# Tile-local attention into a routed mixture of experts: the order of TensorE's work in an attention turn, the way k is read, and the first loads

## The chip, the cores and the metric

One core of a Trainium2 chip runs the whole program. The metric is the device time of one execution in microseconds (us); lower is better. The core has five engines that run their own instruction streams and wait for each other by semaphores: TensorE (PE in the profile, with its weight loads as PEld), VectorE (DVE), ScalarE (ACT), GpSimd (POOL) and SyncE (SP), which here only issues transfers. Sixteen DMA engines carry the transfers.

## The reference

```
# q, k, v: (8, 8, 576, 64); chunks of 64 tokens attend within themselves
scores = matmul(q_c, k_c.T) / sqrt(64)
attn   = exp(scores - max(scores));  attn /= sum(attn) + 1e-9
x      = matmul(attn, v_c)                 -> 4608 tokens x 512
noisy  = x @ w_gate + log1p(exp(x @ w_noise)) * noise
top2   = the two largest of 8 experts per token, softmax over the two
out   += top2_w[k] * (relu(x @ w1[e]) @ w2[e])   for both experts e
```

All tensors are fp32.

## The kernel before, in words

The 4608 tokens are 36 tiles of 128 tokens. A tile is two chunks of 64 tokens for each of 8 heads, and heads go in pairs (hp, 0 to 3). The program has two stages that overlap a little.

**Attention stage.** The function `attend(it)` is one *turn*; turns 0 to 35 each start one tile, and turns 36 to 40 finish the pipeline. A turn is software-pipelined over several tiles. In the program's order it issues on TensorE: `pv(it-2)` (the product of the transposed probabilities with v, L427), `p_trans(it-1)` (four 128x128 transposes of the probabilities, L417), `scores(it+1)` (q times k, L400), `x_trans(it-3)` (four transposes of the finished rows of x, L443). Every fourth turn adds `gate_mm` (L455) and, a turn later, `gate_sum` (L468); the routing of the previous group of tiles adds a few small products (L523, L525) in a step called "pe". The products `scores` and `pv` give 64 rows of the result at a time, so two of them stand side by side in the array (the profile writes 128*64); transposes and `gate_sum` use the full array (128*128), `gate_mm` four columns of 32 (128*32). An fp32 product is two instructions in the trace, a transpose one: x16 for `scores` and `pv`, x4 for the transposes.

VectorE does for each turn the maximum (L405) and the subtraction (L410) for tile it, the three steps of the normalization of tile it-2 (L432, L435, L438), and up to six steps of routing. ScalarE copies the transposed probabilities out of PSUM (L419, inside `p_trans`), does the exponential (L413), copies the transposed x (L449), and the copies and functions of gate and routing. GpSimd scatters finished rows to their experts' slots by indirect DMA (L590); each of the at most two scatters of a turn is held back by a one-element copy (L588) from the maximum or from the reciprocal of that turn. In even turns from 12 to 26 it also splits weights (L125).

PSUM bank use: scores alternate between banks 0 and 1, the transposed probabilities have bank 2, `pv` banks 3 and 4, the transposed x bank 5. So `pv` of the next tile needs the normalization of the last one done, and `scores` of a tile needs the subtraction of the tile two before.

The inputs come in pairs of tiles: `load_qk(j)` and `load_v(j)` fill rings of three buffers (KB, VB, QB). KB holds k in two halves by parity of the head, with zeros in the other rows, so one product does a pair of heads. `scores` reads it as `p k h`: for each key position first the one head, then the other, from two places of the buffer. The scores so stand in PSUM in the order (group, key, head), and VectorE reads them through the view `by_head`. KB and VB are cleared once at the start (L358), before the first loads; the constants are made ahead of that. All loads are issued by SP, in the program's order.

**Expert stage.** From turn 36 on, TensorE runs the blocks of the experts (L267), three tiles of tokens at a time, each product in three parts for precision. Blocks 0 and 1 of expert 0 are gathered early, when the scatters of groups 3 and 6 have landed (`gather`, on SP); the remaining attention and routing turns are woven into block 0 by hooks.

Of the kernel before, what the change touches and what calls it, by code (L numbers as in the profile page):

```python
# [8 lines left out]
FT = mybir.dt.float32  # L9
# [10 lines left out]
P = 128  # L20
# [29 lines left out]
def kernel(ctx, tc, qT, kT, vh, wgn, noise, w1, w2, out, caps=CAPS):  # L50
# [4 lines left out]

    slots = dram.tile([LROWS * NE, ROW], FT, name="slots")
    by_slot = slots.rearrange("(r e) c -> r e c", e=NE)


    jp = consts.tile([P, P], FT, name="jp")  # L60
    nc.gpsimd.iota(jp, pattern=[[1, P]], base=0, channel_multiplier=-1, allow_small_or_imprecise_dtypes=True)
    ident = consts.tile([P, P], FT, name="ident")
    nc.vector.tensor_scalar(ident, jp, 0.0, None, op0=OP.is_equal)
    before = consts.tile([P, P], BF, name="before")
    nc.vector.tensor_scalar(before, jp, 0.0, None, op0=OP.is_gt)
    ones = consts.tile([P, P], BF, name="ones")
    nc.vector.memset(ones, 1.0)
    spacer = consts.tile([1, 1], FT, name="spacer")
    e_row = consts.tile([P, NE], FT, name="e_row")
    nc.gpsimd.iota(e_row, pattern=[[1, NE]], base=0, channel_multiplier=0, allow_small_or_imprecise_dtypes=True)  # L70
    col = consts.tile([P, 1], FT, name="col")
    nc.gpsimd.iota(col, pattern=[[0, 1]], base=0, channel_multiplier=1, allow_small_or_imprecise_dtypes=True)
    slot8 = consts.tile([P, NLIST], FT, name="slot8")
    nc.gpsimd.iota(slot8, pattern=[[NE * P, NLIST]], base=NE - 1, channel_multiplier=NE, allow_small_or_imprecise_dtypes=True)
    tok = consts.tile([P, NT], FT, name="tok")
    nc.gpsimd.iota(tok, pattern=[[P, NT]], base=P, channel_multiplier=1, allow_small_or_imprecise_dtypes=True)

    lii = consts.tile([P, 2, NT], I32, name="lii")
    order = consts.tile([1, NE], I32, name="order")
    cape = consts.tile([P, NE], FT, name="cape")  # L80
    caprow = consts.tile([P, NE], FT, name="caprow")
    top = consts.tile([P, NE], FT, name="top")
    place_e = consts.tile([P, NE], FT, name="place_e")
    for c in sorted(set(caps[1:])):
        n = caps.index(c, 1)
        nc.vector.memset(caprow[:, n:n + caps[1:].count(c)], float(c))
    nc.vector.memset(caprow[:, 0:1], float(caps[0]))
    sel = consts.tile([P, 16], FT, name="sel")
    nc.vector.tensor_add(sel, ident[:, 0:16], ident[:, 32:48])
    nc.vector.tensor_add(sel, sel, ident[:, 64:80])  # L90
    nc.vector.tensor_add(sel, sel, ident[:, 96:112])
    run8 = consts.tile([P, NE], FT, name="run8")
    nc.vector.tensor_copy(run8, e_row)


    wpool = {1: ctx.enter_context(tc.tile_pool(name="weights1", bufs=1))}
# [256 lines left out]
    VB = [vs.tile([P, 2, 2, 2, 4, 65], FT, name=f"vb{n}") for n in range(RING)]  # L353
    QB = {}
    HALF = (slice(0, 64), slice(64, 128))
    for n in range(RING):
        for t in (KB[n], VB[n]):
            (nc.vector if n == 0 else nc.gpsimd).memset(t, 0.0)  # L358

    def load_qk(j):  # L360
        if j < NT // 2:
# [5 lines left out]
    def load_v(j):  # L367
        if j < NT // 2:
            for h in range(2):
                nc.sync.dma_start(VB[j % RING][h::2, h], vh[HALF[h], 2 * j:2 * j + 2])  # L370

    nc.scalar.preload_act_table_set("natural_log_exp_and_others")
    for j in range(2):
        load_qk(j)
        load_v(j)
    wg = consts.tile([P, ND, 32], FT, name="wg")
    nc.sync.dma_start(wg, wgn)
    nz = consts.tile([P, NT, NE], FT, name="nz")
# [7 lines left out]

    PR, PT, XS, XT, RC = {}, {}, {}, {}, {}
    by_head = lambda a: a.rearrange("p (g k h) -> p g h k", g=4, h=2)
    sco = [by_head(PS[:, b, :]) for b in range(2)]

    def x_at(t):
        u, r = divmod(t, 4)
# [4 lines left out]
    def scores(t):  # L397
        for hp in range(4):
            for q in HALF:
                nc.tensor.matmul(PS[q, t % 2, hp * P:(hp + 1) * P], QB[t // 2][:, t % 2, hp, q],  # L400
                                 KB[t // 2 % RING][:, :, t % 2, hp, q].rearrange("p h k -> p k h"), start=True, stop=True)

    def soft_max(t):
        mx = work.tile([P, 4, 2], FT, name="mx", bufs=2)
# [10 lines left out]
    def p_trans(t):  # L415
        for hp in range(4):
            nc.tensor.transpose(PS[:, 2, hp * P:(hp + 1) * P], PR[t][:, hp * P:(hp + 1) * P], ident)  # L417
        PT[t] = work.tile([P, 4, P], FT, name="pts", bufs=2)
        nc.scalar.activation(PT[t].rearrange("p a b -> p (a b)"), PS[:, 2, :], AF.Copy)  # L419

# [241 lines left out]
    def attend(it):  # L662
        STEPS = 6
        if it % 2:
            load_qk((it - 1) // 2 + 3)
        if it % 2 == 0 and it >= 4:
            load_v((it - 4) // 2 + 3)
        if it in (5, 7):
            for r in range(CLEAN + 64 * (it // 2 - 2), CLEAN + 64 * (it // 2 - 1), 16):
                nc.sync.dma_start(slots[r * NE:(r + 16) * NE, 0:USED], zero)  # L670
        if it == 7:
            nc.sync.dma_start(slots[(CLEAN + P) * NE:NLIST * P * NE, CODE:USED].rearrange("(p r) c -> p r c", p=P),
                              zero[:, 0:3 * (NLIST * P - CLEAN - P) // 16].rearrange("p (r c) -> p r c", c=3))
        if it in (9, 11, 13, 15):
            w_load(0, 1, (it - 9) // 2)
        if it == 32:
            zero_out(8)
        if it in (29, 31, 33, 35):
            w_load(0, 2, (it - 29) // 2)
        next_turn()  # L680
        if it == 0:
            scores(0)
        if 0 <= it - 2 < NT:
            pv(it - 2)
        if 0 <= it - 1 < NT:
            p_trans(it - 1)
        if it + 1 < NT:
            scores(it + 1)
        if 0 <= it - 3 < NT:
            x_trans(it - 3)  # L690
        gated = it - 4 >= 0 and (it - 4) % 4 == 3
        if gated:
            gate_mm((it - 4) // 4)
        step_route("pe")
        if it - 5 >= 0 and (it - 5) % 4 == 3:
            gate_sum((it - 5) // 4)
            if grp_of[it - 5] != grp_of.get(it - 4):
                r = route(grp_of[it - 5])
                routing.append([r, next(r)])
        if it < NT:  # L700
            mx = soft_max(it)
            soft_sub(it, mx)
            scatter(1, mx[0:1, 0, 0:1])
            soft_exp(it)
        if 0 <= it - 3 < NT:
            x_copy(it - 3)
        if gated:
            gate_copy((it - 4) // 4)
        step_route("act")
# [12 lines left out]
        if it in range(12, 28, 2):  # L722
            w_split(0, 1, *wq.pop(0), eng=nc.gpsimd)
# [241 lines left out]
```

## Time and profile before

| | |
|---|---|
| median of 3 runs | 1003.32 us (1001.34 to 1003.67) |
| profiled execution | 995.33 us, its span 993.5 us |
| TensorE busy | 970.2 us (98%) |
| VectorE, ScalarE, GpSimd busy | 463.2, 284.0, 225.6 us |
| mean granted TensorE clock | 0.996 |

Times of instructions come from the one profiled execution and count from the start of its span. A row of a timeline has the start, the time from the first start to the last end of what is merged in it, engine, line, operation, output and inputs, shapes and the count; idle time before it and what ended it stand in brackets. Matmuls overlap in the pipeline, so the step from one row's start to the next row's start says more of the cost than a row's own length.

### The profile page before, as it was taken

How to read it: one execution, taken by the hardware profiler on the slowest of the kernel's cores; microseconds unless marked ns; L12 is line 12 of the kernel's file. 1: busy time of each engine (PE TensorE's matmuls, PEld its weight loads, DVE VectorE, ACT ScalarE, POOL GpSimd, SP SyncE). 2: the span in 40 equal slices, each digit the busy share in tenths (PEclk: the TensorE clock that was granted, in tenths of full speed). 3: DMA queues.
4: the chain of work that ended last, by engine and by line, in shares of the span. 5: the costliest groups of instructions: out<-in, count | busy, mean ns of one | idle time of the engine just before them, and what ended most of it. 6: DMA issues, size and time to landing. Idle time of an engine off the chain costs nothing.

```text
span 993.5 us, 16063 instructions
## 1 busy us (share of the span) xinstructions
PE 970.2 (98%) x5788; PEld 853.4 (86%) x5788; DVE 463.2 (47%) x1042; ACT 284.0 (29%) x595; POOL 225.6 (23%) x320
## 2 busy tenths in 40 slices
PE   5999999999999999999999999999999999999996
PEld 4777778798899888988998899889988998899885
DVE  5778876333535442544344434443344334433311
ACT  2556554112233221312231323132213221322100
POOL 3026666831100111021012101210111111111112
PEclk9999999999999999999999999999999999999999
DMA  7989999959621652276116622572264226402213
GB/s 267 311 272 343 317 375 398 293 159 148 177 39 33 148 136 35 36 143 150 36 24 134 164 45 31 103 182 48 32 151 132 47 32 152 112 13 33 32 22 44
DMA packets 96834, 132.92 MB, mean 134 GB/s; under 512 B 23376, under 2 KB 56528, under 8 KB 96752
## 3 DMA queue, kind: packets, MB, share of 16 engines
q1 hardware_dynamic: 80320, 93.54, 31.9%
q0 software_dynamic: 16432, 38.33, 19.3%
q8 instruction: 46, 0.75, 0.3%
q14 instruction: 36, 0.29, 0.1%
HBM read 81.69 MB, written 50.13 MB: 133 GB/s over the span
## 4 chain that ended last, share of the span: by engine, by line
PE 94%; DMA 1%; DVE 1%; issue 1%; POOL 1%; ACT 0%; SPq 0%; POOLq 0%; ACTq 0%
PE PS L267 79%; PE PS L400 5%; PE PS L427 4%; PE PS L417 2%; PE PS L443 2%; PE PS L312 1%; PE PS L455 1%; PE PS L468 1%; DMA slots<-xs,lii 1%; POOL out L234 0%; PE PS L250 0%; DMA kb<-in_kT 0%; POOL slots L590 0%; DMA xg<-slots 0%; DVE xl L258 0%
## 5 line engine op out<-in xcount | busy, mean ns | idle before, releaser
L234 POOL DMA_INDIRECT out<-o,lid x77 | 119.9, 1557 | 662.0 <-DVE o L297 642.3
L267 PE MATMUL PS<-xh,w1h 128*128 128x384 f32 (+2 forms) x768 | 261.7, 341 | 0.5 <-DVE hl L289 0.3
L267 PE MATMUL PS<-xl,w1h 128*128 128x384 f32 (+2 forms) x768 | 260.4, 339 | 0.2 <-DVE xl L258 0.2
L267 PE MATMUL PS<-xh,w1l 128*128 128x384 f32 (+2 forms) x768 | 260.4, 339 | 0.0
L267 PE MATMUL PS<-w2h,hh 128*128 128x512 f32 x584 | 228.6, 392 | 0.0
L267 PE MATMUL PS<-w2h,hl 128*128 128x512 f32 x584 | 228.5, 391 | 0.0
L267 PE MATMUL PS<-w2l,hh 128*128 128x512 f32 x584 | 228.5, 391 | 0.0
L286 ACT ACTIVATE hh<-PS 128x384 fp32r<-128x384 f32 (+2 forms) x192 | 95.2, 496 | 463.0 <-PE PS L267 462.9
L289 DVE SCALAR_TENSOR_TENSOR hl<-PS,hh 128x384 fp32r<-128x384 f32 (+2 forms) x192 | 108.7, 566 | 178.1 <-ACT hh L286 146.4
L297 DVE TENSOR_SCALAR o<-PS,lwt 128x512 f32<-128x512 f32 x77 | 57.7, 749 | 231.1 <-PE PS L267 223.0
L267 PEld LDWEIGHTS PS<-xh,w1h 128*128 128x128 f32 x768 | 144.2, 188 | 7.4 <-issue 4.6
L267 PEld LDWEIGHTS PS<-xl,w1h 128*128 128x128 f32 x768 | 144.2, 188 | 2.1 <-DVE xl L258 0.5
L267 PEld LDWEIGHTS PS<-xh,w1l 128*128 128x128 f32 x768 | 144.2, 188 | 1.0
L267 PEld LDWEIGHTS PS<-w2h,hl 128*128 128x128 f32 x584 | 109.7, 188 | 23.4
L267 PEld LDWEIGHTS PS<-w2h,hh 128*128 128x128 f32 x584 | 109.7, 188 | 22.5
L267 PEld LDWEIGHTS PS<-w2l,hh 128*128 128x128 f32 x584 | 109.5, 188 | 22.7
L590 POOL DMA_INDIRECT slots<-xs,lii x72 | 71.1, 988 | 17.6 <-issue 16.9
L257 ACT ACTIVATE xh<-y 128x512 fp32r<-128x512 f32 x67 | 41.2, 614 | 92.7 <-DVE y L254 92.7
L258 DVE TENSOR_TENSOR xl<-y,xh 128x512 fp32r<-128x512 f32 x67 | 45.0, 671 | 48.2 <-ACT xh L257 48.2
L400 PE MATMUL PS<-kb,qb 128*64 128x128 f32 x576 | 48.8, 315 | 10.1 <-DMA kb<-in_kT 10.1
L400 PEld LDWEIGHTS PS<-kb,qb 128*64 128x64 f32 x576 | 38.3, 143 | 15.9 <-issue 15.4
L254 DVE STREAM_TRANSPOSE y<-xg 128x512 f32<-128x512 f32 x67 | 45.6, 680 | 0.0
(126 smaller groups left out, 692.6 us busy)
## 6 DMA issues: line engine op xcount, KB each, us to landing
st<-in_w SPq DMA_DIRECT2D x36, 512.0 KB
xg<-slots SPq DMA_DIRECT2D x252, 64.0 KB
st<-in_w SPq DMA_DIRECT2D x112, 128.0 KB
out<-zero SPq DMA_DIRECT2D x37, 256.0 KB
vb<-in_vh SPq DMA_DIRECT2D x36, 260.0 KB
qb<-in_qT SPq DMA_DIRECT2D x36, 256.0 KB
kb<-in_kT SPq DMA_DIRECT2D x36, 256.0 KB
xg<-slots SPq DMA_DIRECT2D x9, 256.0 KB
```

Of the source, the lines that this page charges most:

```text
L234: s = nc.gpsimd.indirect_dma_start(out=out, out_offset=bass.IndirectOffsetOnAxis(ap=rows_of(i, j)[0:r], axis=0), in_=o[0:r], in_offset=Non ...
L254: nc.vector.transpose(y[:, 0:4 * r], x[:, 0:4 * r])
L257: nc.scalar.activation(oh, src, AF.Copy)
L258: nc.vector.tensor_sub(ol, src, oh.bitcast(FT))
L267: nc.tensor.matmul(p, a, b, start=first and n == 0, stop=last and n == 2)
L286: nc.scalar.activation(hh[:, 0:n], p, AF.Relu)
L289: nc.vector.scalar_tensor_tensor(hl[:, 0:n], p, 0.0, hh[:, 0:n].bitcast(FT), op0=OP.max, op1=OP.subtract)
L297: nc.vector.tensor_scalar(o[0:r], p[0:r], w, None, op0=OP.mult)
L400: nc.tensor.matmul(PS[q, t % 2, hp * P:(hp + 1) * P], QB[t // 2][:, t % 2, hp, q], KB[t // 2 % RING][:, :, t % 2, hp, q].rearrange("p h k ...
L417: nc.tensor.transpose(PS[:, 2, hp * P:(hp + 1) * P], PR[t][:, hp * P:(hp + 1) * P], ident)
L427: nc.tensor.matmul(PS[q, 3 + hp // 2, o:o + 130], PT[t][:, hp, q], VB[t // 2 % RING][:, :, t % 2, c, hp, :], start=True, stop=True)
L590: s = nc.gpsimd.indirect_dma_start(out=slots, out_offset=bass.IndirectOffsetOnAxis(ap=lii[:, k, t0 + r:t0 + r + 1], axis=0), in_=XS[(t0 + ...
```

## The change

1. In a turn TensorE now does `scores(it+1)`, `pv(it-2)` and, where due, `gate_mm`; then `p_trans(it-1)` and `x_trans(it-3)`; then `gate_sum` and the "pe" step of routing.
2. ScalarE's copy of the transposed probabilities is a function of its own, `p_copy`, and stands behind the exponential of the turn.
3. `scores` reads k as it lies, 64 keys of one head and then 64 of the other, so the scores stand in PSUM as (group, head, key), and the view `sco` follows; the probabilities are still written as (group, key, head).
4. At the start VectorE clears the first tile's half of KB[0], then the second's, then VB[0]; the first pair's q comes by four half-size loads on SP, its k by four on ScalarE's queue; constants are made after that; GpSimd clears KB[1] first and the rest after its constants.

```diff
-    for n in range(RING):
-        for t in (KB[n], VB[n]):
-            (nc.vector if n == 0 else nc.gpsimd).memset(t, 0.0)
...
+    for a in range(2):
+        nc.vector.memset(KB[0][:, :, a], 0.0)
+    nc.gpsimd.memset(KB[1], 0.0)
+    nc.vector.memset(VB[0], 0.0)
+    QB[0] = loads.tile([P, 2, 4, P], FT, name="qb", bufs=RING)
+    for a in range(2):
+        for h in range(2):
+            nc.sync.dma_start(QB[0][h::2, a], qT[HALF[h], a])
+            nc.scalar.dma_start(KB[0][h::2, h, a], kT[HALF[h], a])
     nc.scalar.preload_act_table_set("natural_log_exp_and_others")
-    for j in range(2):
-        load_qk(j)
-        load_v(j)
+    load_v(0)
...
+    nc.gpsimd.memset(VB[1], 0.0)
+    for t in (KB[2], VB[2]):
+        nc.gpsimd.memset(t, 0.0)
+    load_qk(1)
+    load_v(1)
...
-    sco = [by_head(PS[:, b, :]) for b in range(2)]
+    sco = [PS[:, b, :].rearrange("p (g h k) -> p g h k", g=4, h=2) for b in range(2)]
...
-                                 KB[t // 2 % RING][:, :, t % 2, hp, q].rearrange("p h k -> p k h"), start=True, stop=True)
+                                 KB[t // 2 % RING][:, :, t % 2, hp, q], start=True, stop=True)
...
             nc.tensor.transpose(PS[:, 2, hp * P:(hp + 1) * P], PR[t][:, hp * P:(hp + 1) * P], ident)
+
+    def p_copy(t):
         PT[t] = work.tile([P, 4, P], FT, name="pts", bufs=2)
...
+        if it + 1 < NT:
+            scores(it + 1)
         if 0 <= it - 2 < NT:
             pv(it - 2)
-        if 0 <= it - 1 < NT:
-            p_trans(it - 1)
-        if it + 1 < NT:
-            scores(it + 1)
-        if 0 <= it - 3 < NT:
-            x_trans(it - 3)
         gated = it - 4 >= 0 and (it - 4) % 4 == 3
         if gated:
             gate_mm((it - 4) // 4)
-        step_route("pe")
+        if 0 <= it - 1 < NT:
+            p_trans(it - 1)
+        if 0 <= it - 3 < NT:
+            x_trans(it - 3)
...
+        step_route("pe")
         if it < NT:
             mx = soft_max(it)
             soft_sub(it, mx)
             scatter(1, mx[0:1, 0, 0:1])
             soft_exp(it)
+        if 0 <= it - 1 < NT:
+            p_copy(it - 1)
```

TensorE's order in turns 6 and 7 before: L427 is `pv`, L417 `p_trans`, L400 `scores`, L443 `x_trans`.

```order
L427 MATMUL PS<-vb_146,pts 64x130 x8
L417 MATMUL PS<-ident,pr 128x128 x4
L400 MATMUL PS<-kb_141,qb 64x128 x8
L443 MATMUL PS<-ident,xs 128x128 x4
L427 MATMUL PS<-vb_146,pts 64x130 x8
L417 MATMUL PS<-ident,pr 128x128 x4
L400 MATMUL PS<-kb_142,qb 64x128 x8
L443 MATMUL PS<-ident,xs 128x128 x4
L455 MATMUL PS<-xt,wg 32x512 x4
```

The same turns now, to the first transposes of turn 7: L408 is `scores`, L437 `pv`, L465 `gate_mm`, L425 `p_trans`, L453 `x_trans`.

```order
L408 MATMUL PS<-kb_108,qb 64x128 x8
L437 MATMUL PS<-vb_113,pts 64x130 x8
L425 MATMUL PS<-ident,pr 128x128 x4
L453 MATMUL PS<-ident,xs 128x128 x4
L408 MATMUL PS<-kb_109,qb 64x128 x8
L437 MATMUL PS<-vb_113,pts 64x130 x8
L465 MATMUL PS<-xt,wg 32x512 x4
L425 MATMUL PS<-ident,pr 128x128 x4
```

Before, products of 64 columns and transposes of 128 alternate, four changes in a turn; now the two products stand together and the two transposes, two changes in a turn.

ScalarE in two such turns before, with the copy of the probabilities (L419) ahead of the exponential (L413) and the copy of x (L449):

```order
L419 ACTIVATE pts<-PS 128x512
L413 ACTIVATE pr<-pr 128x512
L449 ACTIVATE xt<-PS 128x4x128
L419 ACTIVATE pts<-PS 128x512
L413 ACTIVATE pr<-pr 128x512
L449 ACTIVATE xt<-PS 128x4x128
```

And now, with the exponential (L421) ahead of the two copies (L429, L459):

```order
L421 ACTIVATE pr<-pr 128x512
L429 ACTIVATE pts<-PS 128x512
L459 ACTIVATE xt<-PS 128x4x128
L421 ACTIVATE pr<-pr 128x512
L429 ACTIVATE pts<-PS 128x512
L459 ACTIVATE xt<-PS 128x4x128
```

The exponential and the copy of the probabilities have changed places.

SP's first loads before, to the second pair of tiles (kb_142):

```order
L364 DMA qb<-in_qT 64x1024
L365 DMA kb_141<-in_kT 64x1024
L364 DMA qb<-in_qT 64x1024
L365 DMA kb_141<-in_kT 64x1024
L370 DMA vb_144<-in_vh 64x1040 x2
L364 DMA qb<-in_qT 64x1024
L365 DMA kb_142<-in_kT 64x1024
L364 DMA qb<-in_qT 64x1024
L365 DMA kb_142<-in_kT 64x1024
```

And now, to the second pair (kb_109); the first pair's k is issued by ScalarE, as its first four instructions:

```order
L340 DMA qb<-in_qT 64x512 x4
L331 DMA vb_111<-in_vh 64x1040 x2
L325 DMA qb<-in_qT 64x1024
L326 DMA kb_109<-in_kT 64x1024
L325 DMA qb<-in_qT 64x1024
L326 DMA kb_109<-in_kT 64x1024
```

The first pair's q stands in four halves at the head of SP's queue, and none of SP's first four loads follows a cleared buffer any more.

## Rows read from the trace of the kernel before

**Rows 1.** The page: busy time by engine, and the chain's shares by line.

```profile
PE 970.2 (98%) x5788; PEld 853.4 (86%) x5788; DVE 463.2 (47%) x1042; ACT 284.0 (29%) x595; POOL 225.6 (23%) x320
...
PE PS L267 79%; PE PS L400 5%; PE PS L427 4%; PE PS L417 2%; PE PS L443 2%; PE PS L312 1%; PE PS L455 1%; PE PS L468 1%; DMA slots<-xs,lii 1%; POOL out L234 0%; PE PS L250 0%; DMA kb<-in_kT 0%; POOL slots L590 0%; DMA xg<-slots 0%; DVE xl L258 0%
```

**Rows 2.** Timeline of PE, turns 6 and 7 (start, length, what).

```profile
32.84 1.30 PE L400 MATMUL PS<-kb,qb 128*64 128x128 f32 x16
34.08 0.66 PE L443 MATMUL PS<-ident,xs 128*128 128x128 f32 x4
34.66 1.11 PE L427 MATMUL PS<-vb,pts 128*64 128x130 f32 x16
35.70 0.66 PE L417 MATMUL PS<-ident,pr 128*128 128x128 f32 x4
36.29 1.31 PE L400 MATMUL PS<-kb,qb 128*64 128x128 f32 x16
```

**Rows 3.** Timeline, PE in turn 35, which has no scores.

```profile
145.60 0.66 PE L417 MATMUL PS<-ident,pr 128*128 128x128 f32 x4
...
146.09 0.60 PE L443 MATMUL PS<-ident,xs 128*128 128x128 f32 x4
...
146.62 1.07 PE L455 MATMUL PS<-xt,wg 128*32 128x512 f32 x8
```

**Rows 4.** Lines L400 and L427, matmuls, 29.2 to 145 us (shortest/median/longest ns).

```profile
L400 PE MATMUL PS<-kb,qb x480: 298/300/348, 29.4 to 143.6; 128*64 128x128 f32 x160
...
L427 PE MATMUL PS<-vb,pts x472: 272/273/326, 31.2 to 145.0; 128*64 128x130 f32 x158
```

**Rows 5.** Groups by line, DVE, 30 to 170 us (busy, mean ns | idle before).

```profile
L438 DVE TENSOR_TENSOR xs<-PS,rc 128x512 f32<-128x512 f32 x33 | 22.8, 692 | 1.8 <-DVE rc L435 0.6 <-DMA slots<-xs,lii 0.2
...
L410 DVE TENSOR_TENSOR pr<-PS,mx 128x512 f32<-128x512 f32 x30 | 20.8, 692 | 1.7
```

**Rows 6.** Windows: length, busy PE, PEld, DVE, ACT, POOL, clock, DMA share, GB/s.

```profile
69.59:85.28 15.69, 15.69 (x185) 12.17 (x189) 13.04 (x49) 9.46 (x21) 11.29 (x17) 1.00 0.97 337
...
116.68:132.38 15.70, 15.70 (x186) 12.19 (x189) 12.75 (x51) 8.43 (x19) 10.83 (x19) 1.00 0.99 343
...
150.00:175.00 25.00, 22.85 (x160) 20.09 (x161) 16.64 (x85) 11.72 (x28) 15.83 (x25) 1.00 1.04 396
```

**Rows 7.** Timeline of POOL: two scatters in a row, and a split.

```profile
78.16 1.00 POOL L590 DMA_INDIRECT slots<-xs,lii  x1 [0.16 <-issue]
79.17 0.18 POOL L588 COPY spacer<-rc 1x1 f32<-1x1 f32 x1
79.50 0.99 POOL L590 DMA_INDIRECT slots<-xs,lii  x1 [0.16 <-issue]
...
83.20 1.28 POOL L125 TENSOR_TENSOR w1l<-st,w1h 128x512 fp32r<-128x512 f32 x1
```

**Rows 8.** Timeline of the start: clearing, loads, first scores.

```profile
0.73 0.58 SPq L364 DMA_DIRECT2D qb<-in_qT  x1
...
2.60 1.76 DVE L358 MEMSET kb<- 128x2048 f32 x1
...
4.75 1.79 DVE L358 MEMSET vb<- 128x2080 f32 x1 [0.38 <-issue]
...
10.07 3.68 PE L400 MATMUL PS<-kb,qb 128*64 128x128 f32 x32 [10.07 <-DMA kb<-in_kT]
...
15.27 1.98 PE L400 MATMUL PS<-kb,qb 128*64 128x128 f32 x16
```

**Rows 9.** The chain that ended last: first load, turn 4, last early scatter and gather.

```profile
5.56 4.38 DMA kb<-in_kT
...
24.39 1.04 PE PS L427 x16
...
181.14 5.37 DMA slots<-xs,lii
...
186.53 2.94 DMA xg<-slots
```

**Rows 10.** Timeline of PE around the gather of block 1.

```profile
189.51 0.66 PE L250 MATMUL PS<-ident,xg 128*128 128x128 f32 x4 [2.05 <-DMA xg<-slots]
...
190.25 0.63 PE L267 MATMUL PS<-w2l,hh 128*128 128x512 f32 x1
...
193.65 0.40 PE L267 MATMUL PS<-w2h,hh 128*128 128x512 f32 x1
```

More of the change, by code (lines that the diff above doesn't have):

```diff
@@ L57 @@
     by_slot = slots.rearrange("(r e) c -> r e c", e=NE)
[L60 to L93, printed above, removed]
     wpool = {1: ctx.enter_context(tc.tile_pool(name="weights1", bufs=1))}
@@ new lines @@
+    nc.scalar.preload_act_table_set("natural_log_exp_and_others")
+    load_v(0)
+    jp = consts.tile([P, P], FT, name="jp")
+    nc.gpsimd.iota(jp, pattern=[[1, P]], base=0, channel_multiplier=-1, allow_small_or_imprecise_dtypes=True)
+    ident = consts.tile([P, P], FT, name="ident")
+    nc.vector.tensor_scalar(ident, jp, 0.0, None, op0=OP.is_equal)
+    before = consts.tile([P, P], BF, name="before")
+    nc.vector.tensor_scalar(before, jp, 0.0, None, op0=OP.is_gt)
+    ones = consts.tile([P, P], BF, name="ones")
@@ new lines @@
+    nc.vector.memset(ones, 1.0)
+    spacer = consts.tile([1, 1], FT, name="spacer")
+    e_row = consts.tile([P, NE], FT, name="e_row")
+    nc.gpsimd.iota(e_row, pattern=[[1, NE]], base=0, channel_multiplier=0, allow_small_or_imprecise_dtypes=True)
+    col = consts.tile([P, 1], FT, name="col")
+    nc.gpsimd.iota(col, pattern=[[0, 1]], base=0, channel_multiplier=1, allow_small_or_imprecise_dtypes=True)
+    slot8 = consts.tile([P, NLIST], FT, name="slot8")
+    nc.gpsimd.iota(slot8, pattern=[[NE * P, NLIST]], base=NE - 1, channel_multiplier=NE, allow_small_or_imprecise_dtypes=True)
@@ new lines @@
+    tok = consts.tile([P, NT], FT, name="tok")
+    nc.gpsimd.iota(tok, pattern=[[P, NT]], base=P, channel_multiplier=1, allow_small_or_imprecise_dtypes=True)
+    lii = consts.tile([P, 2, NT], I32, name="lii")
+    order = consts.tile([1, NE], I32, name="order")
+    cape = consts.tile([P, NE], FT, name="cape")
+    caprow = consts.tile([P, NE], FT, name="caprow")
+    top = consts.tile([P, NE], FT, name="top")
+    place_e = consts.tile([P, NE], FT, name="place_e")
+    for c in sorted(set(caps[1:])):
+        n = caps.index(c, 1)
+        nc.vector.memset(caprow[:, n:n + caps[1:].count(c)], float(c))
@@ L376 @@
+    nc.vector.memset(caprow[:, 0:1], float(caps[0]))
+    sel = consts.tile([P, 16], FT, name="sel")
+    nc.vector.tensor_add(sel, ident[:, 0:16], ident[:, 32:48])
+    nc.vector.tensor_add(sel, sel, ident[:, 64:80])
+    nc.vector.tensor_add(sel, sel, ident[:, 96:112])
+    run8 = consts.tile([P, NE], FT, name="run8")
+    nc.vector.tensor_copy(run8, e_row)
+    nc.gpsimd.memset(VB[1], 0.0)
[3 more added lines that the diff above has]
+    load_v(1)
     wg = consts.tile([P, ND, 32], FT, name="wg")
```

## The prediction

> **What bounds the kernel now.** I read the page first: TensorE is busy 98% of the span, and by the chain's shares 79% of it is the expert blocks and some 13% the four parts of the attention turn (5, 4, 2 and 2) [rows 1]. The change touches only the attention stage, so the question is what bounds that stage. TensorE's timeline shows parts that follow each other without a pause, and no row of it carries a wait: from one `scores` to the next 36.29 - 32.84 = 3.45 us [rows 2]. The windows say how near the others are: in a period of four turns, with gate and routing, of 15.69 us, TensorE is busy all the time, VectorE 13.04, ScalarE 9.46, GpSimd 11.29, and the DMA engines move 337 GB/s [rows 6]. So TensorE is the bound, and VectorE is next, not far behind.
>
> **Part 1, the order on TensorE.** By their starts the parts of a turn take: scores 1.24, transposes of x 0.58, `pv` 1.04, transposes of the probabilities 0.59 [rows 2]. Every neighbour in this order is of the other form. Turn 35 has no scores, so its two kinds of transposes stand together; there they take 146.09 - 145.60 = 0.49 and 146.62 - 146.09 = 0.53, and the first matmul's extra length is gone too (0.60 for 0.66) [rows 3]. So leaving a form costs 0.10 and entering one 0.05. It isn't the wait for data: in both places the transposes run without a wait.
>
> The new turn has two changes of form for four. The transposes are as in turn 35: 0.49 + 0.53, which saves 0.15. For scores followed by `pv` no row shows the join. Both are of form 128*64, so the nearest row is that of two transposes: 0.15 less again. The bounds are 0 (each product pays alone) and 0.15. I take 0.15, since those two differ in nothing but the data.
>
> The Trainium skill, "TensorEngine Tiling (Array Packing)", section Key Properties, says that changing the tiling mode, not just the tile, drains TensorE. By it scores to `pv`, both 128x64, is no change, and the saving stands at 0.15; by the 0 above the turn would save 0.15 less. The rows on the transposes agree with it; no run here shows the join of the two products.
>
> The gate's product has a form of its own. It stood between transposes and `pv`, now between `pv` and transposes: two changes either way, nothing saved or lost. `gate_sum` and "pe" are of the transposes' form and stay beside them.
>
> **Part 2, k in runs.** A score matmul lasts 300 ns, one of `pv` 273, though `pv` streams 130 columns and scores 128 [rows 4]. The whole parts differ by 1.24 - 1.04 = 0.20. Weights and form are alike; what differs is that scores take every element from the other half of the buffer, and `pv` takes runs of 65. With runs of 64 I give scores the pace of `pv`: 0.20 saved. Bounds: 0 and 0.21. VectorE's reading of the scores changes from every second element to runs. The subtraction with the step takes 692 ns, the normalization with runs of 64 also 692 [rows 5]: nothing either way.
>
> New turn: 3.45 - 0.15 - 0.15 - 0.20 = 2.95 us. From turn 4 (24.39 [rows 9]) to turn 34 there are 31 full turns: 31 x 0.50 = **15.5 us**, if TensorE stays the bound.
>
> **Part 3, what is late next.** A period of 15.69 becomes 15.69 - 2.0 = 13.7 us on TensorE. VectorE needs 13.04 of it busy, and more with the pause between an operation and one that needs its result. GpSimd: a scatter each 79.50 - 78.16 = 1.34 us, eight in a period, and two splits of 1.28 in the turns that have them [rows 7]: 13.3. The transfers: 337 GB/s x 15.69 us = 5.3 MB, in 13.7 us 386 GB/s; the window after the last turns moves 396 [rows 6]. All three fit, none with room. The copy of the probabilities now stands behind the exponential, which waits for the subtraction; if VectorE is late, that copy is late, and `pv` of the next turn waits for it with everything queued behind it on TensorE. Its slack: `p_trans` is done near the turn's end, then x's transposes and the next scores (0.53 + 0.95) run before `pv` asks. The copy and the exponential before it were hidden beside 0.59 + 1.24 + 0.58, now by less. Bounds for this in the 25 turns with routing (6.2 periods): 0, and 2.0 a period (the whole gain, 12.4). I take 0.3 a period, which puts the period at 14.0: **1.9 us** back. It is nearer to 0, since VectorE's busy time is still below TensorE's.
>
> **Part 4, the start.** Before, k's buffer is cleared from 2.60 to 4.36, the first scores start at 10.07, the second pair's at 15.27 [rows 8]. Now half of the buffer is cleared first: VectorE starts at about 0.7, half of 1.76 is done by 1.6. Two issues of 0.58 on ScalarE follow, and a load lands 2.9 to 4.4 us after its issue [rows 9]: scores at 5.2 to 6.7. They don't set the pace, the second pair does. VB[0] is cleared by 0.7 + 1.76 + 1.79 = 4.3; then SP issues two of v and four of the second pair, the last at 4.3 + 5 x 0.6 = 7.3, landing at 10.2 to 11.7. I take 11.0, which is 4.3 earlier. By then `p_trans(0)` was done in the old order and is still to do in the new one (about 1 us at the slow clock of this phase: 1.98 for a score part against 1.31 later [rows 2, 8]). So turn 4 starts **3.2 us** earlier; bounds 1.5 and 4.3. Constants that move behind the clearing are ready before the first transposes want them; GpSimd's later clearing is of buffers wanted after 11 us.
>
> **Part 5, the way into the experts.** TensorE waits 2.05 us for the gather of block 1, and its products then take 0.63 for 0.40 until 193.65 [rows 10]. Before that stand the scatter (5.37) and the gather (2.94) [rows 9]. The scatters are bound to turns and hooks and come earlier with them, but the window before runs the DMA engines at 1.04 of their time and 396 GB/s [rows 6], and the turns that end in it give up 5 x 0.50 us. So the gather may wait for transfers: 0 to 2.5 us, or gain up to 2 if the wait and the slow products go. I take **1 us** lost.
>
> **Sum.** Against the profiled 995.33 us: -3.2 - 15.5 + 1.9 + 1.0 = -15.8, so 979.5. The timed runs have their median 8 us above the profiled one; I put the same difference on it: 1003.3 - 15.8 = **987.5 us**.
>
> **Rivals.**
> - *TensorE keeps the pace alone.* No turn waits, and the start gives 4.3: -4.3 - 15.5 + 0.5 = -19.3, 984. For it: VectorE's 13.04 is below 13.7. Against: a service with so little room seldom costs nothing.
> - *Half is lost to the next bound.* VectorE, GpSimd or the transfers hold the period at 14.9 or more, or one of the two savings (join of the products, runs of k) isn't there: 5 to 9 us less, -7 to -11: 992 to 996. For it: 13.0, 13.3 and 386 of 396 all at once. Against: buffers two and three deep between the engines.
> - *The gather is not earlier.* If scatters and zeroes keep the DMA engines at 396 GB/s all the way, the gather lands when it did, and TensorE waits out what it gained: 1003. For it: DMA share 1.04. Against: before turn 30 the rate is 337, so there was room.
> - *The clock falls.* If TensorE, with its transposes in one run and with more short waits, were granted 1.2 GHz in part of the stage, a turn there costs 2.95 x 1.98 / 1.31 = 4.5 us for 3.45. It decides once more than a third of the turns run so (1.55 lost against 0.50 gained); all of them give 31 x 1.0 - 3 = +28: 1031. Against: the clock was 1.00 in every window of turns with the same transposes [rows 6]. The Trainium skill, "TensorE: Matmul & The Clock Gate", section "Part 4: PE-mode transpose", says that transposes don't count as work for the clock; by it a longer run of them speaks for this rival, and the windows so far do not.
>
> **How the numbers follow.** Forecast 0.54, its own range 984 to 992; TensorE alone 0.18; half lost 0.18; gather pinned 0.06; clock 0.04. The range 982 to 996 holds the forecast, nearly all of the first rival and most of the second, and leaves out the last two. A measurement of this kernel tells about 0.3% (3 us) from no change: faster 0.54 + 0.18 + 0.18 = 0.90, same 0.06, slower 0.04.
>
> **What would show it.** In a plain turn TensorE's rows should start 0.95 (scores), 0.99, 0.49, 0.53 apart, a score matmul should last 273 ns, and `pv` behind scores should have no longer first matmul. Periods of four turns should take 13.7 to 14.2 us, with VectorE above 90%. Waits of `pv` for ScalarE's copy that add to more than 0.5 us a period would mean that the new place of the copy decides; score matmuls still at 300 ns, that the runs were not the cause; first scores later than 8 us, that the start is wrong. The prediction is wrong altogether if TensorE's wait at block 1's gather grows beyond 5 us.

## The result, and the profile after

The changed kernel takes 993.89 us (median of 4 runs, 992.28 to 995.48), the kernel before 1002.84 beside it (4 runs): ratio 0.9912, 95% interval 0.9892 to 0.9933. So it is 8.95 us faster, where 15.8 were forecast; 993.89 lies inside 982 to 996, but where the rival "half is lost to the next bound" put it. Its profiled execution took 993.54 us (span 991.7).

The page, busy time and chain, answering [rows 1]:

```profile
PE 959.4 (97%) x5788; PEld 850.6 (86%) x5788; DVE 463.9 (47%) x1043; ACT 282.5 (28%) x595; POOL 225.8 (23%) x320
...
PE PS L231 81%; PE PS L437 3%; PE PS L408 3%; PE PS L425 2%; PE PS L453 1%; PE PS L465 1%; PE PS L276 1%; DVE xs L448 1%; PE PS L478 1%; DMA kb<-in_kT 0%; POOL out L198 0%; DVE mx L413 0%; PE PS L214 0%; DVE pr L418 0%
```

TensorE's timeline in a plain turn, answering [rows 2] (L425 transposes of probabilities, L453 of x, L408 scores, L437 `pv`):

```profile
41.11 0.66 PE L425 MATMUL PS<-ident,pr 128*128 128x128 f32 x4
41.60 0.60 PE L453 MATMUL PS<-ident,xs 128*128 128x128 f32 x4
42.13 1.09 PE L408 MATMUL PS<-kb,qb 128*64 128x128 f32 x16
43.06 1.06 PE L437 MATMUL PS<-vb,pts 128*64 128x130 f32 x16
44.05 0.66 PE L425 MATMUL PS<-ident,pr 128*128 128x128 f32 x4
```

The starts are 0.49, 0.53, 0.93 and 0.99 apart, in all 2.94 us; 0.49, 0.53, 0.95 and 0.99 were forecast, so the turn itself came out. The windows, one to a period of four turns, show what became of it later (columns as in [rows 6]):

```profile
34.51:48.25 13.74, 13.74 (x178) 11.44 (x178) 10.36 (x35) 7.78 (x18) 0.00 (x0) 1.00 0.96 316
48.25:61.90 13.65, 13.65 (x183) 11.59 (x183) 11.52 (x39) 9.01 (x22) 2.64 (x3) 1.00 1.01 393
61.90:80.18 18.28, 16.02 (x183) 12.47 (x183) 13.90 (x49) 9.28 (x22) 11.87 (x18) 0.91 0.94 331
80.18:96.07 15.89, 14.81 (x184) 12.00 (x183) 13.63 (x52) 9.71 (x22) 9.85 (x16) 1.00 0.82 272
```

13.7 us holds for two periods. Once GpSimd is busy with scatters (its column, 11.87) three periods are longer than the 15.7 of the kernel before: 18.3 and 15.9 here, then 16.0; the next two are 15.5 and 14.6. TensorE is no longer busy all the time. One such place in the timeline of all engines (scatter L600, exponential L421, its transposed copy L429, reciprocal's input L442):

```profile
71.28 1.11 PE L437 MATMUL PS<-vb,pts 128*64 128x130 f32 x16
...
72.27 0.99 POOL L600 DMA_INDIRECT slots<-xs,lii  x1 [0.16 <-issue]
...
72.32 0.65 PE L425 MATMUL PS<-ident,pr 128*128 128x128 f32 x4
...
73.65 1.09 PE L408 MATMUL PS<-kb,qb 128*64 128x128 f32 x16 [0.23 <-DVE pr L418]
73.69 0.98 POOL L600 DMA_INDIRECT slots<-xs,lii  x1 [0.25 <-issue]
75.19 0.60 ACT L429 ACTIVATE pts<-PS 128x512 f32<-128x512 f32 x1 [0.94 <-remote]
75.21 0.17 DVE L442 TENSOR_SCALAR rc<-PS 128x8 f32<-128x8 f32 x1 [1.62 <-remote]
...
76.48 0.92 PE L437 MATMUL PS<-vb,pts 128*64 128x130 f32 x6 [1.74 <-DVE gsm L543]
```

`pv` is done at 72.39, the transposes at 72.97. VectorE (L442 needs that `pv`) has nothing else to do from 73.59 on, ScalarE (L429 needs those transposes) from 74.26 on. Yet both start at 75.2: 2.8 and 2.2 us after the work that they wait for, of which they idle 1.62 and 0.94. I call this a late signal. The trace also notes when TensorE's semaphore was counted up: three times in a row, at 75.11, 75.17 and 75.23, for parts that were done at 72.39, 72.97 and 73.41. By these records it is the signal that is late, and not the engines that wait for it. TensorE then waits 1.74 us for the normalization behind L442.

### The profile page after: what moved, and what is told of

It reads as the page before. It is cut to its first block, busy times and chain, and to the rows that moved or that the text cites. A ratio compares the mean times of both kernels' runs of the same rounds, so it can differ in the third digit from the quotient of the medians.

```text
span 991.7 us, 16057 instructions
## 1 busy us (share of the span) xinstructions
PE 959.4 (97%) x5788; PEld 850.6 (86%) x5788; DVE 463.9 (47%) x1043; ACT 282.5 (28%) x595; POOL 225.8 (23%) x320
## 4 chain that ended last, share of the span: by engine, by line
PE 92%; DVE 4%; issue 2%; DMA 0%; POOL 0%; ACT 0%; another core or an unknown queue 0%; SPq 0%; DVEq 0%; POOLq 0%
PE PS L231 81%; PE PS L437 3%; PE PS L408 3%; PE PS L425 2%; PE PS L453 1%; PE PS L465 1%; PE PS L276 1%; DVE xs L448 1%; PE PS L478 1%; DMA kb<-in_kT 0%; POOL out L198 0%; DVE mx L413 0%; PE PS L214 0%; DVE pr L418 0%
## 5 line engine op out<-in xcount | busy, mean ns | idle before, releaser
L600 POOL DMA_INDIRECT slots<-xs,lii x72 | 72.5, 1007 | 18.5 <-issue 17.9
L408 PE MATMUL PS<-kb,qb 128*64 128x128 f32 x576 | 43.2, 295 | 10.9 <-DMA kb<-in_kT 9.6
L408 PEld LDWEIGHTS PS<-kb,qb 128*64 128x64 f32 x576 | 34.0, 146 | 16.0 <-issue 13.0
L437 PE MATMUL PS<-vb,pts 128*64 128x130 f32 x576 | 40.2, 280 | 6.6 <-DVE gsm L543 1.7
```

What stands on the lines that cost most here:

```text
L437: nc.tensor.matmul(PS[q, 3 + hp // 2, o:o + 130], PT[t][:, hp, q], VB[t // 2 % RING][:, :, t % 2, c, hp, :], start=True, stop=True)
L600: s = nc.gpsimd.indirect_dma_start(out=slots, out_offset=bass.IndirectOffsetOnAxis(ap=lii[:, k, t0 + r:t0 + r + 1], axis=0), in_=XS[(t0 + ...
```

## The experiments

The runs were taken in sessions, each on one chip with the kernel before beside it. The sessions fall into two groups that must be kept apart: in group A (the result above and the runs under "What holds the turns with scatters") the kernel before has a median of 1001.9 to 1002.8 us, in group B (all other runs) of 993.2 to 993.6. Group B is three sessions on three chips; the second session of group A had a fourth, and the chip of the result is not noted. Times and ratios are compared inside a group.

**The kernel before again (group B).** No edit.

> The kernel before once more, as a kernel of its own. Its profiled execution took 995.3 us while its timed runs took 1001 to 1004. If that execution was an unusually quiet one, a new trace shows waits of TensorE in the turns with scatters (none of its periods of four turns showed one: 15.69 to 15.72 us each), periods above 15.7 there or a lower clock, and a total near 1003. If the quiet trace is the usual one, the periods stay at 15.7, the trace takes 995 again and the 8 us lie somewhere that these rows do not show. Ratio to itself 1.000.

993.39 us (12 runs), ratio 1.0005 (0.9993 to 1.0018). Its periods are those of [rows 6]. The 995.33 of the prediction's trace lies within the range of these runs and of those beside them (991.1 to 995.4) and outside those of group A (999.3 to 1004.4). So it was most likely taken in a session like group B's, and the 8 us in the prediction lie between sessions, not between profiled and timed runs. One of its windows, turns 16 to 19:

```profile
67.25:82.94 15.69, 15.69 (x182) 12.19 (x181) 13.03 (x49) 9.46 (x21) 11.36 (x17) 1.00 0.97 339
```

**Each part alone (group B).** The order, with the copy behind the exponential (body of the turn):

```
 pv(it - 2) | p_trans(it - 1) | scores(it + 1) | x_trans(it - 3) | gate_mm | "pe"     (before)
 scores(it + 1) | pv(it - 2) | gate_mm | p_trans(it - 1) | x_trans(it - 3) | "pe"     (alone)
...
 soft_exp(it)
+p_copy(it - 1)
```

> The kernel before with the new order of the turn alone (and the copy of the probabilities behind the exponential); k is still read by every second element, the start is the old one. Theory of the prediction (TensorE's pace is all that counts): 31 turns x 0.30 = 9.3 us less, periods of four turns of 14.5 us with and without scatters. Theory of the next bound (from the first scatters on something else holds a period at 15.5 to 16 whatever TensorE needs): 14.5 only in turns 4 to 11, 8 x 0.30 = 2.4 us less, and waits of pv or scores from turn 12 on. Theory of the copy's place (waits come from the new order itself): the same waits, and a gain near 2 us, while the run with k in runs alone has none.

987.30 us, ratio 0.9932 (0.9914 to 0.9950): 6.1 less. Every period with scatters is 14.5, TensorE busy all through; one of them:

```profile
64.24:78.73 14.49, 14.49 (x183) 12.56 (x182) 12.28 (x50) 9.37 (x21) 11.37 (x19) 1.00 0.97 344
```

(15.70 - 14.50) / 4 = 0.30 us a turn, to the hundredth what two changes of form less were worked out to give. The copy's new place costs nothing in these periods.

The reading of k in runs alone:

```
-KB[t // 2 % RING][:, :, t % 2, hp, q].rearrange("p h k -> p k h")
+KB[t // 2 % RING][:, :, t % 2, hp, q]
-sco = [by_head(PS[:, b, :]) for b in range(2)]
+sco = [PS[:, b, :].rearrange("p (g h k) -> p g h k", g=4, h=2) for b in range(2)]
```

> The kernel before with k read in runs by head alone; order and start are the old ones. Theory of the prediction: a score matmul lasts 273 ns for 300, scores 1.04 us for 1.24, 31 x 0.20 = 6.2 us less, periods of 14.9 us all through. Theory of the next bound: 14.9 in turns 4 to 11 alone, then 15.5 or more with waits, 1.6 us less in all. Theory of the copy's place: no waits, the full 6.2 us, since the order is the old one.

988.31 us, ratio 0.9950 (0.9932 to 0.9967): 5.0 less. The score matmuls by line (shortest, median, longest ns), answering [rows 4], and two periods:

```profile
L400 PE MATMUL PS<-kb,qb x464: 272/273/323, 30.0 to 135.2; 128*64 128x128 f32 x155
```

```profile
79.51:94.64 15.13, 14.91 (x183) 11.57 (x182) 13.07 (x52) 9.59 (x21) 9.83 (x16) 1.00 0.95 335
109.68:124.53 14.85, 14.85 (x182) 11.55 (x181) 12.76 (x53) 8.44 (x19) 10.76 (x19) 1.00 0.99 354
```

273 ns for 300: reading in runs was the cause, and a period is 0.85 to 0.57 shorter.

The start alone (half a buffer cleared first, first loads of k on ScalarE's queue by single tiles, constants behind):

```
+for a in range(2):
+    for h in range(2):
+        nc.sync.dma_start(QB[0][h::2, a], qT[HALF[h], a])
+        nc.scalar.dma_start(KB[0][h::2, h, a], kT[HALF[h], a])
...
```

> The kernel before with the new start alone (first pair cleared and loaded by single tiles, constants behind it); order and k's form are the old ones. From the trace of the changed kernel, whose second pair's scores start at 13.29 us for 15.27 and whose turn 4 starts at 22.81 for 24.39: about 2 us less. Theory of the prediction: 3.2 us less, since the new order delays the first transposes by about 1 us and the old one does not; then turn 4 starts near 21.5 to 22.4. If a later wait (the gather of block 1) absorbs it: nothing.

993.62 us (12 runs), ratio 0.9998 (0.9985 to 1.0011): nothing. TensorE's timeline here, and then of the kernel before in the same session (second pair's scores, and `pv` of turn 4):

```profile
6.41 3.68 PE L408 MATMUL PS<-kb,qb 128*64 128x128 f32 x32 [6.41 <-DMA kb<-in_kT]
...
13.12 1.98 PE L408 MATMUL PS<-kb,qb 128*64 128x128 f32 x16 [1.46 <-DMA kb<-in_kT]
...
21.48 1.11 PE L435 MATMUL PS<-vb,pts 128*64 128x130 f32 x16
```

```profile
9.64 3.68 PE L400 MATMUL PS<-kb,qb 128*64 128x128 f32 x32 [9.64 <-DMA kb<-in_kT]
...
14.65 1.31 PE L400 MATMUL PS<-kb,qb 128*64 128x128 f32 x16
...
22.06 1.11 PE L427 MATMUL PS<-vb,pts 128*64 128x130 f32 x16
```

The first scores gain 3.2 us, the second pair's 1.5, and turn 4 only 0.6: TensorE waits 1.46 for the second pair's load and does its scores in 1.98 us, where the kernel before, which starts them later, needs 1.31. The clock goes with that: the first granted clock that the traces note, at full speed, begins at 15.86 us here and at 14.41 in the kernel before. At the last gate product this run is 1.8 us ahead (156.3 for 158.1), but the expert products behind the gather come 2.7 later (196.2 for 193.5): in these two traces the way into the experts takes the gain back, as the last of the expected readings has it.

**What holds the turns with scatters (group A).** Four runs: the changed kernel again; the same with the old start; with a cheaper maximum; with narrow scatters. The changed kernel again, without an edit:

> The changed kernel once more, beside the kernel before on the same chip. Order alone and runs of k alone kept TensorE without waits (14.50 and 14.85 to 15.13 us a period), so both together should give 13.7; its first trace has 13.65 until the scatters begin and then 17.6, 16.1, 16.5, 15.5, 14.6, with stretches of 1 to 2 us in which every engine idles. If that first trace is a mishap of one execution, the periods are now 13.7 to 14.2 and the time is some 980. If it is the kernel's habit, the periods with scatters are 15 to 17 again, TensorE waits 7 to 9 us in turns 12 to 34, and the ratio is 0.99 to 1.00.

995.40 us for 1001.91 before, ratio 0.9935 (0.9915 to 0.9954). The late signals are back, 1.7 to 3.1 us behind `pv` in five turns, the first two at the same places of the program. The periods with scatters are 16.7, 17.1 and 16.8, then 14.5 and 15.1.

The old start:

```
-(the start above)
+for n in range(RING):
+    for t in (KB[n], VB[n]):
+        (nc.vector if n == 0 else nc.gpsimd).memset(t, 0.0)
+for j in range(2):
+    load_qk(j)
+    load_v(j)
```

> The changed kernel with the start of the kernel before (all buffers cleared first, pairs loaded whole, no load on ScalarE's queue): order and runs of k are in. If the two together hit the next bound by themselves: periods of 13.7 before and 15 to 17 after the first scatters, as in the changed kernel, and the same time within 2 us, since the new start alone measured nothing. If the new start (ScalarE's own load queue, later clearing of the third buffers) brings the waits: periods of 13.7 to 14.2 all through and 11 to 13 us less than before (0.300 + 0.2 us a turn, less what the gather of block 1 keeps).

997.17 us, ratio 0.9951 (0.9932 to 0.9970); periods 16.7, 17.1 and 15.9, then 14.9 and 16.1. The late signals come without the new start too.

The cheaper maximum:

```
-nc.vector.tensor_reduce(mx, sco[t % 2], AX.X, OP.max)
+nc.vector.tensor_reduce(mx, sco[t % 2][:, :, :, 0:16], AX.X, OP.max)
```

> The changed kernel with the maximum taken over the first 16 keys of each head for all 64 (any shift gives the same softmax): VectorE's reduction falls from 0.68 to about 0.2 us, some 1.9 us a period of four turns less on VectorE; TensorE, ScalarE, GpSimd and the transfers are as they are. If VectorE is the next bound (12.2 to 13.2 us of work and 0.7 to 0.9 of short gaps in a period of 13.65): the periods with scatters fall to 13.7 to 13.9, no wait over 0.3 us is left on TensorE in turns 12 to 34, the kernel takes some 6 to 10 us less than the changed one. If transfers are the bound, or late semaphores have another cause: periods of 15 to 17 and waits as before.

997.28 us, ratio 0.9953 (0.9935 to 0.9970). VectorE is busy 10.7 to 11.6 us of a period, for 12.3 to 13.9 in the changed kernel beside it, and the periods stay:

```profile
47.07:60.72 13.65, 13.65 (x184) 11.59 (x182) 10.06 (x41) 9.26 (x21) 1.84 (x2) 1.00 0.99 382
60.72:78.28 17.56, 14.80 (x183) 12.38 (x181) 11.45 (x48) 9.15 (x21) 12.33 (x19) 0.95 0.97 348
```

VectorE, which the prediction named as next in line, is not what holds these periods.

The narrow scatters:

```
...
-in_=XS[(t0 + r) // 4][:, r % 4, 0:USED], in_offset=None)
+in_=XS[(t0 + r) // 4][:, r % 4, DM:USED], in_offset=None)
...
```

> The changed kernel with scatters of 3 columns for 515 (12 bytes a row for 2060), the expert blocks reading rows of q in place of the scattered rows, which leaves out the moving of the tokens to their experts; only the attention stage is to be read. The number of scatters, GpSimd's time for each and every engine's work stay; the bytes in a period fall from about 5.3 to 3.2 MB, in 13.7 us 235 GB/s for 386. If transfers are the next bound: periods of 13.7 to 14.0 in turns 12 to 34 and no stretch in which all engines idle. If VectorE is the next bound: periods of 15 or more as in the changed kernel.

One execution, 992.18 us. With 192 to 270 GB/s in place of 270 to 351 the periods are still 15.0 to 16.1 and late signals still come:

```profile
92.10:108.00 15.90, 14.40 (x181) 11.86 (x181) 11.74 (x47) 9.05 (x21) 9.16 (x15) 1.00 0.61 192
```

The scatters' bytes are not the cause either.

**Who issues, and when (group B).** Plain transfers from SyncE in place of GpSimd's scatters:

```
...
-nc.gpsimd.tensor_copy(spacer, gate)
-s = nc.gpsimd.indirect_dma_start(out=slots, out_offset=..., in_=XS[...])
+row = ((t0 + r) * 2 + k) * P
+nc.sync.dma_start(slots[row:row + P, 0:USED], XS[(t0 + r) // 4][:, r % 4, 0:USED])
...
```

> The changed kernel with every scatter of the attention turns and of the first two blocks as a plain transfer of the same 264 KB from SyncE's queue to fixed rows, in place of GpSimd's indirect transfer; the expert blocks read rows of q and codes made up on GpSimd, which leaves out the moving of the tokens to their experts. All work of TensorE, VectorE and ScalarE in the turns stays, and so do the bytes. What is seen in the changed kernel: signals of TensorE's finished parts that reach VectorE and ScalarE 1 to 3 us late, each time while GpSimd issues indirect transfers 1.35 us apart. If these issues are the cause: periods of 13.7 to 14.0 all through turns 12 to 34, no late signal, no stretch in which ScalarE waits 4 us for a finished product in the first expert block. If the pace of TensorE with the bytes is the cause, whoever issues them: periods of 15 to 17 as before.

One execution, 984.15 us for 993.63 before. Periods of 13.64, 13.77, 13.63 and 13.65, no late signal; then one of 19.17, in which a normalization (L447) waits 5.0 us for transfers. I first took the even periods as proof that GpSimd's issues bring the late signals. They are not: the last run below keeps these issues and has the same periods. The plain transfers were not run in group A, where the late signals are.

The scatters released later:

```
 mx = soft_max(it); soft_sub(it, mx)
-scatter(1, mx[0:1, 0, 0:1])
 soft_exp(it)
+scatter(1, PR[it][0:1, 0:1])
...
-scatter(1, RC[it - 2][0:1, 0, 0])
 norm_c(it - 2)
+scatter(1, XS[(it - 2) // 4][0:1, (it - 2) % 4, 0:1])
```

> The changed kernel with the two scatters of a turn released about 0.7 us later each: the first by the exponential in place of the maximum, the second by the normalized rows in place of the reciprocal's input. The same work on every engine. If the late signals depend on where in TensorE's turn GpSimd issues (the scatters that precede them start in scores, pv and the first transposes), the periods of 15 to 17 change clearly: to 13.7 to 14.5 when the new phases are clear of it, and the kernel takes 4 to 8 us less than the changed one (ratio to before 0.982 to 0.988). If only the number of issues counts, periods and time stay within 2 us (0.992).

988.22 us for 993.63, ratio 0.9946 (0.9928 to 0.9963). No late signal, periods of 14.05, 13.91, 14.58, then two waits of TensorE. The chain behind the longer one names its cause, and the waits of VectorE give its size (in all, times, longest):

```profile
113.53 6.24 DMA slots<-xs,lii
119.82 0.70 DVE xs L448
...
120.66 1.28 PE PS L437 x16
```

```profile
DVE xs L448 <- DMA slots<-xs,lii: 5.4, 2, 4.0
```

A scatter lands 6.24 us after its issue, and the normalization of a group's first turn waits for it: it takes over the buffer of the group five back, and the pool gives a buffer free when all eight scatters of that group have landed (in the traces this instruction waits for eight semaphores, with the fixed tiles below for two).

**The buffers of normalized rows as fixed tiles (group B).**

```
-rows = last_rows.enter_context(tc.tile_pool(name="rows", bufs=5, side="right"))
+rows = last_rows.enter_context(tc.tile_pool(name="rows", bufs=1, side="right"))
+XR = [rows.tile([P, 4, 520], FT, name=f"xs{n}") for n in range(5)]
-XS[u] = rows.tile([P, 4, 520], FT, name="xs")
+XS[u] = XR[u % 5]
```

With the later gates:

> The later gates, and the five buffers of normalized rows as five fixed tiles: the rows of a turn then wait only for the two scatters of the turn 20 before that used the same quarter, instead of all eight scatters of that group (no more memory, the same work). With the later gates alone two waits were left, 4.0 us at 120.7 and 1.9 us at 136.9, both behind a normalization that waits for scatters to land. If these are all that is left: periods of 13.7 to 14.3 through turn 34, the last gate product some 5 us earlier than with the gates alone (near 146.5), and 2 to 5 us less in time, since the gather of block 1 may keep part: ratio to before 0.990 to 0.992. If the transfers (386 GB/s needed) are late everywhere: another wait takes the place, for k, q or v, and the ratio stays at 0.995.

983.84 us for 993.19, ratio 0.9901 (0.9884 to 0.9919). VectorE's waits for scatters are gone, and it gains 9.4 us where the gates alone gained 5.4; periods 14.04, 13.77, 14.57, 14.09.

With the changed kernel's own gates (the "fixed-tile run" from here on):

> The changed kernel with the five fixed tiles alone, its gates as they are. The normalization's wait for scatters is the smaller cause there: if the late signals of TensorE's parts decide, periods of 15 to 17 and the time stay (ratio 0.992 to 0.996) and signals come 1 to 3 us late as often as in the changed kernel. If the waits were the normalization's all along and only put down to late signals by the trace, periods fall to 13.7 to 14.5 as with both edits.

982.11 us for 993.19, ratio 0.9886 (0.9867 to 0.9906): the best of all, and against my expectation, for not one signal is late:

```profile
61.07:74.77 13.70, 13.70 (x184) 11.68 (x182) 12.33 (x50) 9.37 (x21) 11.31 (x18) 1.00 1.00 381
...
88.41:102.06 13.65, 13.65 (x183) 11.68 (x182) 12.35 (x49) 9.37 (x22) 9.59 (x15) 1.00 0.97 356
102.06:115.70 13.64, 13.64 (x184) 11.71 (x182) 12.38 (x50) 8.34 (x20) 10.87 (x18) 1.00 1.00 376
```

The place that answers to the late signal above, in the timeline of this run:

```profile
71.01 0.83 PE L438 MATMUL PS<-vb,pts 128*64 128x130 f32 x12
...
71.53 0.99 POOL L601 DMA_INDIRECT slots<-xs,lii  x1 [0.16 <-issue]
71.77 0.66 PE L426 MATMUL PS<-ident,pr 128*128 128x128 f32 x4
...
72.44 0.15 DVE L443 TENSOR_SCALAR rc<-PS 128x8 f32<-128x8 f32 x1
...
73.10 0.58 ACT L430 ACTIVATE pts<-PS 128x512 f32<-128x512 f32 x1
```

Both engines take the parts up as soon as they are through with what stood before (72.52 and 73.19). Up to turn 22 this kernel is the changed one, instruction for instruction, and the late signals of group A begin in turns 16 and 18. So the fixed tiles cannot have removed those. All five traces of group A have them; of the eight kernels in group B none has one of over 0.5 us. They go with the session, as does the slower kernel before. What the fixed tiles remove is the wait for the scatters, which comes in from turn 22.

What causes the late signals was not settled, and two suspects are left. One is GpSimd's issues, in sessions like group A's: in the two traces of the changed kernel all ten signals that VectorE gets over 1 us late come 0.4 to 0.7 us behind the end of a scatter's issue (74.67 and 75.11 in the case above). The other is the recording of the profile itself. From 60 to 150 us the changed kernel's trace holds 122 records of VectorE's semaphore for 196 instructions that count it, the fixed-tile run's 212 for 219; before 60 us, ahead of the scatters, neither lacks one. The other four traces of group A lack as many.

## Why the prediction was right and wrong

**Parts 1 and 2 were right, together and apart.** Order alone gives 0.30 a turn, runs alone 0.14 to 0.21; together, where nothing interferes, a period is 13.65, 2.05 less where 2.0 was worked out. In the fixed-tile run the gate product of turn 35 follows that of turn 7 after 95.4 us, before after 108.5: 28 turns x 0.47. The join of scores and `pv`, which no row of before showed, takes nothing: `pv` has 0.99 us there, as forecast with the full 0.15 saved. The Trainium skill, "TensorEngine Tiling (Array Packing)", section Key Properties, says that a change of the tiling mode drains TensorE; scores and `pv` have one mode, and the rows agree.

**Part 3 failed: the step that named VectorE as next and priced a period's loss at 0.3 us.** It compared busy times, and these were no limit: the fixed-tile run loses nothing with VectorE busy 12.4 of 13.65, and a cheaper maximum helped nothing where periods were long. The copy's place, which I had named as the thing to watch, did not decide either: it holds `pv` up once in the fixed-tile run, for 0.3 us. In the changed kernel the profile puts 2.9 us of `pv`'s waits in these periods to ScalarE, but at the two longest, before 125.48 and 140.11, VectorE's normalization ends last (125.33 and 139.97), behind the copy (124.68 and 139.89).

From the gate product of turn 15 to that of turn 35 the changed kernel takes 80.3 us in group A, the fixed-tile run 68.0 in group B. In those 12.3 us are late signals, a stretch of lower clock behind the second of them (0.91 in its window), and some of a wait that stood in the program and that I hadn't looked for: a normalization behind eight scatters. They were not taken apart further; VectorE's waits there show only this for the scatters:

```profile
DVE xs L448 <- DMA slots<-xs,lii: 0.8, 1, 0.8
```

In the kernel before it is 0.2 us [rows 5]. Faster turns reach a buffer sooner while a scatter takes longer to land; with later gates that wait came to 5.4 us.

**Part 4 was mis-sized:** 3.2 forecast; the new start alone brings 0.6 at turn 4 in its session and nothing in time. The second pair's load landed at 13.1 and not 11.0, and the reach of the slow clock wasn't in the sum: what starts earlier runs at 1.98 us a part for 1.31. That reach also differs between executions of one kernel: in the trace that the prediction used, the first noted clock, at full speed, begins at 19.54 and `pv` of turn 4 at 24.3, in the second trace of the kernel before at 14.41 and 22.1. So a single trace could not price the start to better than 2 us.

**Part 5 was mis-sized, 1.0 for 5.0.** The chain of waits of the kernel before (first) and of the fixed-tile run (second), both of group B, answering [rows 9]:

```profile
179.81 4.28 DMA slots<-xs,lii
184.11 3.23 DMA xg<-slots
...
187.38 0.66 PE PS L250 x4
188.04 2.75 PE PS L267 x12
```

```profile
164.67 6.60 DMA slots<-xs,lii
171.29 4.50 DMA xg<-slots
...
175.83 1.12 PE PS L214 x4
176.95 3.74 PE PS L231 x12
```

The last early scatter is issued 15.1 us sooner. It lands 2.3 slower and the gather 1.3 slower, so TensorE gets the block 11.5 sooner, after a wait of 4.8 us for 1.3; then its four transposes and twelve products take 1.5 longer, at the lower clock level for part of them (0.75 of full speed in the mean from 177 to 181 us). 15.1 - 3.6 - 1.5 leaves 10.0, and over the last 693 us of the program the runs with indirect scatters differ by no more than 0.4. The slower landing goes with busier transfers, in the 4 us behind the scatter's issue (kernel before first):

```profile
180.00:184.00 4.00, 4.00 (x20) 3.30 (x19) 0.75 (x1) 0.00 (x0) 3.47 (x7) 1.00 0.70 262
```

```profile
165.00:169.00 4.00, 4.00 (x19) 3.34 (x18) 0.75 (x1) 0.00 (x0) 3.47 (x7) 1.00 1.03 374
```

In the kernel before the DMA engines had a share of 0.70 by then, in the fixed-tile run they are still at 1.03. Part 5 named this and then took 1 us, when its own bound was 2.5 and its rival "the gather is not earlier" stood beside it. Against the same trace, between the last gate product and the products near 290 us, order alone lost 3.7 us and runs alone 2.2. These sizes hang on that one trace of the kernel before, the fastest of its runs: against the trace that the prediction used, where TensorE waits 2.05 for the gather and then runs at the lower clock level, the fixed-tile run loses 2.6 there for 5.0. That the hand-over takes back more than 1 us is shown by both, how much is not.

**The sum and the base.** In group B the terms are, for the fixed-tile run: start and turns, to the last gate product, -15.1 (forecast -16.8), way into the experts +5.0 (forecast +1.0); against the prediction's trace -16.4 and +2.6. Both sums lie 1 to 3 us off the 11.1 us that the timed runs give. The three parts alone, 6.1 + 5.0 + 0, add to these 11.1 us. The base of 1003.3 beside a trace of 995.3 most likely put a time of group A on a trace of group B; that difference was no constant to be carried over. The kernel before loses some 9 us in group A as well; where was not traced, so it isn't shown that late signals take them.

That 993.89 fell inside the range is in part luck. The base fitted because the result came from group A as well, and the loss came in part from things that no term held: late signals of that session and a wait behind scatters.

Of the rivals, "half is lost" gave the time, though VectorE and the scatters' bytes, two of the three bounds that it named, did not hold the period, and both savings are there; the third, GpSimd, is not cleared, by its issues if not by its busy time. "The gather is not earlier" was part of it. The clock did not fall with the two kinds of transposes standing together: 1.00 in every period of the fixed-tile run, and below 1 in all the traces only behind waits of TensorE. The Trainium skill, "TensorE: Matmul & The Clock Gate", section "Part 4: PE-mode transpose", spoke for that rival; no row here bears it out.

The changed kernel with its own buffers was not run in group B. What the wait for scatters costs it there stays open; its gain would be expected between the 5.4 us of the later gates and the 11.1 of the fixed tiles, but that was not measured.

## What to carry to other kernels

Price a faster stage at its two ends too: what it waits for at the next hand-over is set by transfers that don't get faster, and here a sixth to a third of the gain went there. A pool's buffer comes free only when its last reader is done; fixed tiles, tracked by the part that is written, freed each quarter by itself and took no more memory. And before a trace and a time are put together, see that they are of one session: running the kernel before again, as a kernel of its own, showed that these were not. An effect that is seen in one session has to be tested in that session.

## What the runs showed of the hardware

- Signals of finished parts on TensorE reached idle engines late in two sessions (72.39 to 75.21 above; up to 3.1 us in the changed kernel, 3.5 with the cheaper maximum), with fewer bytes and with less on VectorE too. No kernel of the three sessions of group B had one over 0.5 us, the fixed-tile run with the same instructions up to turn 22 among them. While scatters run, the traces of the two sessions also lack some two fifths of VectorE's and ScalarE's semaphore records.
- Scores and `pv` with other weights and other data, but of one form, join for nothing (0.99 us for `pv`); two changes of form less in a turn are 0.30 us.
- Taking its 128 columns alternately from two places of a buffer costs an fp32 matmul 300 ns, for 273 when it reads them in runs of 64.
- A scatter of 264 KB lands 4.3 us after its issue at a DMA share of 0.70, 6.6 at 1.03.
